# Cosine attention and a GELU layer on one core: a new split of one batch's fill, and two row reductions one step sooner

## The chip, the cores and the metric

The kernel runs on one core of a Trainium2 chip. The core has a matrix engine (TensorE, PE in the profile), a vector engine (VectorE, DVE), an engine for tabulated functions (ScalarE, ACT), a general engine (GpSimd, POOL) and a queue engine (SyncE, SP) that here issues transfers. Each engine takes its own list of instructions in order, and waits on semaphores where an instruction needs another engine's result. The metric is the time of one execution on the device in microseconds; of several executions the median counts. Before the change five executions took 416.24 to 417.19 us, median 416.77 us.

## The reference

Eight batches of 12 heads, 448 positions, 64 numbers a head. Queries and keys are divided by their length, the scores by tau (0.1), then softmax and the product with v. The result, 3584 rows of 768, goes through a layer of 2048 with the exact GELU and back to 768.

```python
q_n = q / (np.linalg.norm(q, axis=-1, keepdims=True) + 1e-06)
k_n = k / (np.linalg.norm(k, axis=-1, keepdims=True) + 1e-06)
scores = np.matmul(q_n, k_n.transpose(0, 1, 3, 2)) / tau
attn = np.exp(scores - np.max(scores, axis=-1, keepdims=True))
attn = attn / (np.sum(attn, axis=-1, keepdims=True) + 1e-09)
x = np.matmul(attn, v)          # (8, 12, 448, 64) -> (3584, 768)
h = x @ w_in                    # (3584, 2048)
g = 0.5 * h * (1.0 + erf(h / sqrt(2)))
out = g @ w_out                 # (3584, 768)
```

## The kernel before

**Units of work.** Four heads of one batch are a quad; there are three quads to a batch and 24 in all, numbered through. The first batch (b = 0) has quads 0 to 2, the second (b = 1) 3 to 5, the third 6 to 8. A list of units holds quad 0 in two halves and then each quad whole, so that unit u + 4 with u = 4 in the second batch means "up to and with quad 6", and u + 5 "up to and with quad 7".

**What a quad goes through.** `load_qk` (issued on SP, four buffers) brings q and k in float32. `square` on GpSimd multiplies them with themselves (two buffers `sq`). `reduce` (L165, VectorE) sums the squares of each row into `nq`; quads 6 and 7 share one `nq` tile, and so do the later steps on it. `logs` and `roots` (ScalarE) take the root as exp(0.5 ln), `inverses` (GpSimd, then VectorE, L192) the inverse, `scale` (GpSimd, L208) multiplies it into q and k and makes bfloat16, and `transposes` turns the result: for most quads by a transposing transfer issued on SP (L220). Then come seven passes of `scores` (PE, L246, four matmuls each, into one of three pairs of PSUM banks called st0, st1, st2) and `exps` (ScalarE, L253, one activation each), which also free the pair again. `both` finishes a quad: `sums` (PE, L275, into a single PSUM bank), `turned` (VectorE, L297, tile `tr`), `inverted` and `spread` (VectorE, L309 to L318), `values` (PE, L289), `normalise` (VectorE, L323, tile `x`).

**The layer behind it.** `first(b)` multiplies the batch's 448 rows with w_in (PE, L649, tiles `hp`) and takes the GELU (ScalarE, L685). The product with w_out is cut into pieces: a piece is one matmul of 384 columns (L352, tile `op`), 16 pieces make one half of an output tile, and the sixteenth also issues its copy out of PSUM on VectorE (L356, tile `ot`), after the second half the store on SP too. These pieces are a `fill`: they are kept and put between the passes of the next batch's attention, to give PE work while ScalarE takes exponentials. The second batch's attention has 96 pieces, of three output tiles: first halves of tiles 0, 1, 2, then second halves of 0, 1, 2. Below they are ot0, ot1, ot2, in that order twice.

**Banks.** Two single PSUM banks, `mm0` and `mm1`, are taken in turn by each new `op` tile and by the first `hp` tiles of `first`. From the second batch on `sums` takes the bank whose turn is next, without passing the turn on; so the tile that comes after takes the same bank, and must wait until `turned` has read the sums.

**The order around the change.** It is written out by hand in `attention(b, fill)`: `run()` issues the next part of the fill by the numbers of `plan`, `visit(b, pairs)` issues passes of scores and exponentials into the named pairs, and `upto(f, n)` issues step f for all units below n that have not had it yet. In the second batch the order is:

- (at the end of `first(0)`: three passes), run 1, scale and transposes of quad 5, loads, square of quad 6, three passes
- run 2, three passes
- run 3, a load, two passes, square of quad 7
- run 4, three passes, `both` of quad 3, loads, two passes, reduce of quad 6
- run 5, three passes, `both` of quad 4, two passes, reduce of quad 7, logs and roots of quads 6 and 7
- run 6, `both` of quad 5, inverses, and then `first(1)`

In the later batches the same code runs, but `first(b - 1)` has already reduced up to and with unit u + 3, so that only one reduction is left for attention, where the first of its two `upto(reduce, ...)` calls issues it.

Of the kernel before, what the change touches and what calls it, by code (L numbers as in the profile page):

```python
# [16 lines left out]
def kernel(  # L17
# [151 lines left out]
    def logs(n):  # L169
        nq = nq_t.pop(n)  # L170
        ln_t[n] = nrm.tile(list(nq.shape), F32, tag="lq", name=f"lq{n}")
        nc.scalar.activation(ln_t[n], nq, AF.Ln, bias=tiny)

    def roots(n):
        ln = ln_t.pop(n)
        if n <= NQ:
            sr_t[n] = root2[n % len(root2)][:, :math.prod(shapes[n])]
            nc.scalar.activation(sr_t[n][:, :, 0], ln.rearrange("p j i s c -> p (j i s c)"), AF.Exp, scale=0.5)
        else:
            sr_t[n] = nrm.tile(list(ln.shape), F32, tag="sr", name=f"sr{n}")  # L180
            nc.scalar.activation(sr_t[n], ln, AF.Exp, scale=0.5)  # L181

    def inverses(n):
        sr = sr_t.pop(n)
        shape = [128] + shapes[n]
        se = nrm.tile(shape, F32, tag="se", name=f"se{n}")
        if n <= NQ:
            nc.vector.tensor_reduce(se.rearrange("p j i s c -> p (j i s c)"), sr, mybir.AxisListType.X, ALU.add)
        else:
            nc.gpsimd.tensor_scalar(se, sr, 1e-6, None, ALU.add)  # L190
        rn = nrm.tile(shape, F32, tag="rn", name=f"rn{n}")
        nc.vector.reciprocal(rn, se)  # L192
        rn_t[n] = rn
# [42 lines left out]
    def scores(g, banks, p=None):  # L236
        qkT = qkT_t[g]
        if p is None:
            p = st_turn[0]
            st_turn[0] ^= 1  # L240
        st = pair(p, f"st{g}_{banks[0][1]}")
        for n, (s, c) in enumerate(banks):
            rows = slice(64 * s, 64 * (s + 1))
            for h in range(2):
                cols = slice(64 * h, 64 * (h + 1))
                nc.tensor.matmul(st[cols, n, :S], lhsT=qkT[rows, 1, c, cols], rhs=qkT[rows, 0, :, cols],  # L246
                                 start=True, stop=True, tile_position=(64 * s, 64 * h))
        st_t[g, banks[0]] = st

    def exps(g, banks):  # L250
        st, m = st_t.pop((g, banks[0])), len(banks)
        pt = ptp.tile([128, 2, S], BF16, tag="pt", name=f"pt{g}_{banks[0][1]}")
        nc.scalar.activation(pt[:, :m], st[:, :m, :S], AF.Exp, scale=inv_tau)  # L253
        for n, (s, c) in enumerate(banks):
            pt_t[g, s, c] = pt[:, n]
# [69 lines left out]
    def both(g, p):  # L325
        sums(g)
        turned(g)
        inverted(g)
        spread(g, 0)
        spread(g, 1)  # L330
        values(g, p=p)
        normalise(g, 0)
        normalise(g, 1)
# [9 lines left out]
    def second_pieces(sb, t, ni):  # L343
        state = {}

        def mm(kf):
            if kf == 0:
                state["ps"] = mm_tile(f"op{sb}_{t}_{ni}")
                if ni == 0:
                    ot_t[sb, t] = op_.tile([128, d_model], F32, tag="ot", name=f"ot{sb}_{t}")  # L350
            ps, ot = state["ps"], ot_t[sb, t]
            nc.tensor.matmul(ps[:, :NH], lhsT=g_t[sb][:, kf, t * 128:(t + 1) * 128],  # L352
                             rhs=wo[:, kf, ni * NH:(ni + 1) * NH],
                             start=(kf == 0), stop=(kf == KF - 1))
            if kf == KF - 1:
                nc.vector.tensor_copy(ot[:, ni * NH:(ni + 1) * NH], ps[:, :NH])  # L356
                if ni == 1:
                    store(sb, t, ot, 0, d_model, (nc.sync, nc.sync))

        return [lambda kf=kf: mm(kf) for kf in range(KF)]  # L360
# [33 lines left out]
    def upto(f, n, last=None):  # L394
        last = {load_qk: NG, load_v: NV, root: len(groups), load_wi: 4, load_wo: 4}.get(f, NU)
        while done.get(f, 0) < min(n, last):
            done[f] = done.get(f, 0) + 1
            f(done[f] - 1)
# [180 lines left out]
    def visit(b, pairs):  # L579
        for p in pairs:  # L580
            n, c = passes[at.get(b, 0)]
            at[b] = at.get(b, 0) + 1
            scores(b * NQ + n, ((0, c), (1, c)), p)
            exps(b * NQ + n, ((0, c), (1, c)))

    def attention(b, fill):
        fill = list(fill)
        plan = {96: (16, 14, 16, 18, 16, 16), 128: (20, 18, 20, 22, 32, 16)}[len(fill)]
        parts = iter(plan)

        def run():
            for _ in range(next(parts)):
                fill.pop(0)()

        x_t[b] = xp.tile([128, KD, S], BF16, tag="x", name=f"x{b}")
        g0, u = b * NQ, b * NQ + 1
        run()
        upto(scale, u + 3)
        upto(transposes, u + 3)
        if b == 1:  # L600
            upto(load_qk, g0 + NQ + 2)
            upto(square, u + 4)
        visit(b, (0, 1, 2))
        if b > 1:
            upto(scale, u + 4)
            upto(transposes, u + 4)
        run()
        visit(b, (0, 1, 2))
        run()
        upto(load_qk, g0 + NQ + 3)  # L610
        visit(b, (0, 1) if b <= 2 else (0, 1, 2))
        upto(square, u + 5)
        run()
        visit(b, (0, 1, 2))
        both(g0, 0)
        upto(load_v, b + 3)
        upto(load_qk, g0 + NQ + 4)
        visit(b, (1, 2))
        upto(reduce, u + 4 + (b > 1))
        run()  # L620
        visit(b, (1, 2, 0))
        both(g0 + 1, 1)
        visit(b, (2, 0))
        upto(reduce, u + 5)
        n = 2 * b + 4
        if n < len(groups):
            logs(n)
            roots(n)
        run()
        both(g0 + 2, 2)  # L630
        if n < len(groups):
            inverses(n)
            done[root] = n + 1
            if b > 1:
                visit(b + 1, (0, 1))
# [72 lines left out]
    fill = []  # L708
    for b in range(B):
        if b == 0:  # L710
            attention_first()
            acc.close()
            third.append(ctx.enter_context(tc.tile_pool(name="ps_third", bufs=1, space=bass.MemoryType.PSUM)))
        else:
            attention(b, fill)
        first(b)
        sb, hf = divmod(b, 2)
        todo = [(t, ni) for t in (range(3) if hf == 0 else range(3, 7)) for ni in range(2)]
        if b == 0:
            todo.sort(key=lambda x: x[1])  # L720
        tail = [2 * S // 128 - 1] if b == B - 1 else []
        fill = [f for t, ni in todo if t not in tail for f in second_pieces(sb, t, ni)]
        fill += [f for t in tail for f in last_pieces(sb, t)]
# [37 lines left out]
```

## Time and profile before

The profiled execution took 416.24 us; the span on the page, from the first to the last instruction, is 414.4 us. The granted clock of PE was 1.000 over the span.

| | us |
|---|---|
| median of five executions | 416.77 |
| the profiled execution | 416.24 |
| its span | 414.4 |
| PE busy | 406.3 |
| ACT busy | 246.2 |
| DVE busy | 188.6 |
| POOL busy | 166.9 |
| one reduce of a whole quad (L165), in the chain | 1.92 |
| one square of a whole quad (L156) | 3.17 |
| one exponential pass (L253), mean | 0.917 |
| 96 pieces (L352) in the chain | 15.60 |
| q and k loads on SP, issue to landing, median | 6.9 and 8.8 |

How to read the lines: in an order of time a line gives the start and the length in us, the engine, the source line and operation, the tile written, an arrow, the tiles read, the shapes, and how many instructions of the kind stand together; in square brackets is the idle time of the engine before them and what ended it. In a list of waits a line gives who waited for whom: us in total, times, the longest. A busy PE is not a PE at its peak; its idle time is what a better order can take away.

### The profile page before, as it was taken

What the parts mean: (1) busy time and instruction counts of PE and PEld (TensorE: products, weight loads), DVE (VectorE), ACT (ScalarE), POOL (GpSimd) and SP (SyncE); (2) the same over time, 40 slices, a digit from 0 to 9 for tenths busy, and PEclk for the clock granted to TensorE, in tenths of its full rate; (3) what the DMA queues carried; (4) which work ended last, traced back from release to release, by engine and by line L of the source; (5) the groups of instructions that cost most, each with busy time, mean ns of one, the idle gap of its engine ahead of it and who ended that gap; (6) DMA issues with size and microseconds to landing.
All of it is one profiled execution on the core that took longest, in us unless ns stands there. A gap on an engine that the chain in (4) does not pass through costs nothing.

```text
span 414.4 us, 8256 instructions
## 1 busy us (share of the span) xinstructions
PE 406.3 (98%) x3506; PEld 212.3 (51%) x3506; DVE 188.6 (45%) x379; ACT 246.2 (59%) x358; POOL 166.9 (40%) x113
## 2 busy tenths in 40 slices
PE   7999999899999999999999999999999999999996
PEld 3445545455555555555555555555555555545564
DVE  5687116923268221943148431783118611481021
ACT  6995686546746567754764648755665467754300
POOL 4998605074820919044630537217370233000000
PEclk9999999999999999999999999999999999999999
DMA  8999999625396405935296232965078120510033
GB/s 289 262 260 206 203 241 300 136 57 133 57 225 205 115 19 92 278 91 125 30 201 217 65 107 46 210 195 133 2 144 217 40 44 2 120 40 2 0 78 77
DMA packets 66516, 54.53 MB, mean 132 GB/s; under 512 B 38576, under 2 KB 61488, under 8 KB 66480
## 3 DMA queue, kind: packets, MB, share of 16 engines
q1 hardware_dynamic: 53984, 41.79, 38.3%
q0 software_dynamic: 12112, 11.80, 17.9%
q8 instruction: 27, 0.44, 0.4%
q10 hardware_dynamic: 384, 0.43, 0.4%
q14 instruction: 9, 0.07, 0.1%
HBM read 45.61 MB, written 11.01 MB: 137 GB/s over the span
## 4 chain that ended last, share of the span: by engine, by line
PE 92%; DVE 4%; ACT 2%; DMA 1%; issue 0%; POOL 0%; DVEq 0%
PE hp L649 35%; PE op L352 33%; PE st L246 9%; PE o L289 7%; PE sm L275 4%; PE op L367 1%; DVE nq L165 1%; PE sm L266 1%; ACT pt L253 1%; PE tp L225 1%; DMA qk<-in_q_dram 1%; DVE x L323 1%; PE spin L403 0%; DVE tr L297 0%; DVE tr L309 0%
## 5 line engine op out<-in xcount | busy, mean ns | idle before, releaser
L253 ACT ACTIVATE pt<-st 128x896 bf16<-128x896 f32 x168 | 142.8, 917 | 66.5 <-PE st L246 66.2
L649 PE MATMUL hp<-x,wi 128*128 128x448 bf16 x768 | 146.8, 353 | 1.2 <-DVE tr L297 1.2
L352 PE MATMUL op<-wo,g 128*128 128x384 bf16 x864 | 147.8, 326 | 0.0
L352 PEld LDWEIGHTS <-g 128*128 128x128 bf16 x864 | 81.5, 98 | 62.1 <-issue 10.7
L649 PEld LDWEIGHTS <-wi 128*128 128x128 bf16 x768 | 74.5, 98 | 72.5 <-issue 4.0
L685 ACT ACTIVATE g<-hp 128x448 bf16<-128x448 f32 x128 | 65.9, 545 | 68.3 <-PE hp L649 68.0
L208 POOL TENSOR_TENSOR qkb<-qk,rn 128x896 bf16<-128x896 f32 (+1 forms) x49 | 79.7, 1652 | 38.0 <-DVE rn L192 37.9
L356 DVE COPY ot<-op 128x384 f32<-128x384 f32 x54 | 29.6, 548 | 101.6 <-PE op L352 101.6
L165 DVE TENSOR_REDUCE nq<-sq 128x28 f32<-128x1792 f32 (+2 forms) x30 | 48.8, 1636 | 53.1 <-POOL sq L156 50.4
L156 POOL TENSOR_TENSOR sq<-qk 128x1792 f32<-128x1792 f32 (+1 forms) x22 | 66.5, 3037 | 14.0 <-DMA qk<-in_k_dram 14.0
L190 POOL TENSOR_SCALAR se<-sr 128x28 f32<-128x28 f32 (+1 forms) x14 | 4.3, 310 | 127.6 <-ACT sr L181 127.5
L246 PE MATMUL st<-qkT 64*64 64x448 bf16 x672 | 48.0, 358 | 0.8 <-ACT pt L253 0.4
L289 PE MATMUL o<-pt,v 64*64 64x448 bf16 x672 | 36.9, 352 | 0.0
L246 PEld LDWEIGHTS <-qkT 64*64 64x64 bf16 x672 | 18.5, 105 | 24.7 <-issue 16.3
L318 DVE STREAM_TRANSPOSE rs<-rc 128x448 f32<-128x448 f32 x48 | 28.1, 623 | 0.8
L323 DVE TENSOR_TENSOR x<-o,rs 128x448 bf16<-128x448 f32 x48 | 27.0, 599 | 1.0 <-DVE rs L318 0.5
L289 PEld LDWEIGHTS <-v 64*64 64x64 bf16 x672 | 17.7, 106 | 17.0 <-issue 8.4
L192 DVE RECIPROCAL rn<-se 128x28 f32<-128x28 f32 (+2 forms) x18 | 6.8, 376 | 42.8 <-POOL se L190 42.6
L297 DVE STREAM_TRANSPOSE tr<-sm 128x448 f32<-128x448 f32 x24 | 15.5, 646 | 14.2 <-PE sm L275 11.1
L275 PE MATMUL sm<-pt,ones 128*32 128x448 bf16 (+1 forms) x336 | 17.8, 332 | 0.0
L309 DVE TENSOR_REDUCE tr<-tr 32x28 f32<-32x28 f32 x84 | 16.4, 196 | 1.6
L275 PEld LDWEIGHTS <-ones 128*32 128x32 bf16 x336 | 6.8, 95 | 9.0 <-issue 7.2
(43 smaller groups left out, 118.1 us busy)
## 6 DMA issues: line engine op xcount, KB each, us to landing
out_dram<-ot SPq DMA_DIRECT2D x54, 192.0 KB, 3.3
qk<-in_q_dram SPq DMA_DIRECT2D x23, 448.0 KB, 6.9
qk<-in_k_dram SPq DMA_DIRECT2D x23, 448.0 KB, 8.8
v<-in_v_dram POOLq DMA_DIRECT2D x7, 672.0 KB, 12.2
wi<-in_moe_w_in_dram POOLq DMA_DIRECT2D x8, 384.0 KB, 13.9
wo<-in_moe_w_out_dram POOLq DMA_DIRECT2D x4, 768.0 KB, 14.1
qk<-in_q_dram SPq DMA_DIRECT2D x2, 224.0 KB, 3.4
v<-in_v_dram POOLq DMA_DIRECT2D x1, 448.0 KB, 8.2
```

The source lines that it names most:

```text
L156: eng.tensor_tensor(sq[:, part], t[:, part], t[:, part], ALU.mult)
L165: nc.vector.tensor_reduce(nq[:, part], sq[:, part], mybir.AxisListType.X, ALU.add)
L208: eng.tensor_tensor(qkb[:, i, :, s0:s1].rearrange("p c s d -> p s c d"), t[:, i, s0:s1], rn[:, i].to_broadcast([128, s1 - s0, C, D]), ALU. ...
L246: nc.tensor.matmul(st[cols, n, :S], lhsT=qkT[rows, 1, c, cols], rhs=qkT[rows, 0, :, cols], start=True, stop=True, tile_position=(64 * s, 6 ...
L253: nc.scalar.activation(pt[:, :m], st[:, :m, :S], AF.Exp, scale=inv_tau)
L275: nc.tensor.matmul(bank_t[g, "sm"][r:r + 32, cols], lhsT=ones, rhs=pt_t[g, s, c][:, cols], start=(c < 2), stop=(c >= C - 2), tile_position ...
L289: nc.tensor.matmul(bank_t[g, h][cols, :S], lhsT=v_t[g][rows, s, c, :], rhs=pt_t[g, s, c][rows], start=(c == 0), stop=(c == C - 1), tile_po ...
L323: nc.vector.tensor_tensor(x_t[b][:, 2 * n + h, :], bank_t.pop((g, h))[:, :S], rs_t.pop((g, h)), ALU.mult)
L352: nc.tensor.matmul(ps[:, :NH], lhsT=g_t[sb][:, kf, t * 128:(t + 1) * 128], rhs=wo[:, kf, ni * NH:(ni + 1) * NH], start=(kf == 0), stop=(kf ...
L356: nc.vector.tensor_copy(ot[:, ni * NH:(ni + 1) * NH], ps[:, :NH])
L649: nc.tensor.matmul(hps[m], lhsT=wi[:, kd, m * 128:(m + 1) * 128], rhs=x_t[b][:, kd, :], start=(kd == 0), stop=(kd == KD - 1))
L685: nc.scalar.activation(g_t[sb][:, m, hf * S:(hf + 1) * S], hps.pop(m), AF.Gelu)
```

## The change

Two edits in `attention`. The fill of the second batch is split 20, 13, 14, 17, 16, 16 instead of 16, 14, 16, 18, 16, 16; batches with 128 pieces, and the other batches with 96, keep their numbers. And the row sums of squares: `upto(reduce, u + 4)` is called ahead of `upto(square, u + 5)`, before the fourth run, and `upto(reduce, u + 5)` where the first of the two calls stood; the last call falls away. In the second batch quad 6 is so reduced between the copies of ot1 and ot2 (first halves), and quad 7 where quad 6 was, between quad 3's `normalise` and the second copy of ot1. In the later batches the new call has nothing left to issue, and the other issues the same as before at the same place.

```diff
     def attention(b, fill):
         fill = list(fill)
-        plan = {96: (16, 14, 16, 18, 16, 16), 128: (20, 18, 20, 22, 32, 16)}[len(fill)]
-        parts = iter(plan)
+        if len(fill) == 128:
+            parts = iter((20, 18, 20, 22, 32, 16))
+        else:
+            parts = iter((20, 13, 14, 17, 16, 16) if b == 1 else (16, 14, 16, 18, 16, 16))
...
         visit(b, (0, 1) if b <= 2 else (0, 1, 2))
+        upto(reduce, u + 4)
         upto(square, u + 5)
         run()
         visit(b, (0, 1, 2))
...
         visit(b, (1, 2))
-        upto(reduce, u + 4 + (b > 1))
+        upto(reduce, u + 5)
         run()
         visit(b, (1, 2, 0))
         both(g0 + 1, 1)
         visit(b, (2, 0))
-        upto(reduce, u + 5)
```

## The prediction

> **What bounds the kernel now.** I read the page's first two parts, then TensorE's (PE's) waits, then the order of time in the second batch's attention, where every edit acts, engine by engine.
>
> ```profile
> PE 406.3 (98%) x3506; PEld 212.3 (51%) x3506; DVE 188.6 (45%) x379; ACT 246.2 (59%) x358; POOL 166.9 (40%) x113
> ...
> PE 92%; DVE 4%; ACT 2%; DMA 1%; issue 0%; POOL 0%; DVEq 0%
> ```
>
> PE is busy for 406.3 of 414.4 us, and the chain that ended last is 92% PE. A change can only gain what PE waits. TensorE's waits in the whole span:
>
> ```profile
> PE spin L403 <- DVE root L89: 1.9, 1, 1.9
> PE hp L649 <- DVE tr L297: 1.2, 1, 1.2
> PE st L246 <- ACT pt L253: 0.4, 1, 0.4
> ```
>
> The first is the start. The other two both lie in the second batch (46 to 84 us); after 81.09 us PE waits for nothing. In order of time, PE first:
>
> ```profile
> 54.70 0.72 PE L246 MATMUL st<-qkT 64*64 64x448 bf16 x8
> 55.85 0.38 PE L246 MATMUL st<-qkT 64*64 64x448 bf16 x4 [0.43 <-ACT pt L253]
> 56.17 2.45 PE L352 MATMUL op<-wo,g 128*128 128x384 bf16 x14
> ...
> 65.48 0.76 PE L246 MATMUL st<-qkT 64*64 64x448 bf16 x12
> ```
>
> and from the third quad's sums on:
>
> ```profile
> 78.40 1.52 PE L289 MATMUL o<-pt,v 64*64 64x448 bf16 x28
> 81.09 3.19 PE L649 MATMUL hp<-x,wi 128*128 128x448 bf16 x16 [1.17 <-DVE tr L297]
> ```
>
> So after its first fill PE waits for the third exponential, and at the end of the attention for VectorE's transpose of the last sums (tr5; quads are numbered through, so the second batch has 3, 4, 5 and the third batch begins with 6, 7). VectorE (DVE):
>
> ```profile
> 62.99 0.56 DVE L356 COPY ot<-op 128x384 f32<-128x384 f32 x1 [2.65 <-PE op L352]
> 65.59 0.56 DVE L356 COPY ot<-op 128x384 f32<-128x384 f32 x1 [2.04 <-PE op L352]
> 67.07 0.65 DVE L297 STREAM_TRANSPOSE tr<-sm 128x448 f32<-128x448 f32 x1 [0.93 <-PE sm L275]
> ...
> 78.02 2.00 DVE L165 TENSOR_REDUCE nq<-sq 128x28 f32<-128x1792 f32 x1
> 79.94 0.54 DVE L356 COPY ot<-op 128x384 f32<-128x384 f32 x1
> 80.40 0.63 DVE L297 STREAM_TRANSPOSE tr<-sm 128x448 f32<-128x448 f32 x1
> ```
>
> VectorE has slack up to 67 us and then runs without a pause to tr5; the reductions of quads 6 and 7 (71.37 and 78.02 us) stand in that stretch. GpSimd (POOL), which makes what they reduce:
>
> ```profile
> 61.18 3.17 POOL L156 TENSOR_TENSOR sq<-qk 128x1792 f32<-128x1792 f32 x1 [11.56 <-DMA qk<-in_k_dram]
> 66.81 3.17 POOL L156 TENSOR_TENSOR sq<-qk 128x1792 f32<-128x1792 f32 x1 [2.45 <-DMA qk<-in_k_dram]
> ```
>
> The squares of quad 6 end at 64.35 us (61.18 + 3.17): their k arrives late. This line decides the forecast.
>
> **Part one, the fills.** The first run goes from 16 to 20 pieces; the sums after each run go from 16, 30, 46, 64 to 20, 33, 47, 64. A piece is one matmul with 384 columns, 0.1625 us (96 take 15.60 us in the chain). PE would come to the scores at 54.70 + 4 × 0.1625 = 55.35 us. The third pair of scores needs the third exponential, which ends at 55.81 us whatever PE does (53.27 + 2.54, after a table load that nothing here moves), so it starts at 55.85 as before, and the second run at about 56.2 as before, with four pieces more behind it: 0.65 us gained. One small price: quad 4's transposed tile lands at 46.36 + 12.3 = 58.66 us, its first scores would move from 58.85 to 58.68, and may lose up to 0.1 us, before a point that will turn out to have slack. With 64 pieces done after four runs either way, PE would come to the sums of quad 3 (sm3) at 66.24 - 0.65 = 65.59 us. Nothing else is moved past a queue by the fills; the eviction of the second piece group (ot1) falls into run two, at some 58.3 us instead of 59.78.
>
> **Part two, the reductions.** On VectorE the built order becomes: copy ot1, reduce 6, copy ot2, copy ot0 (second half), tr3 to x3, reduce 7, copy ot1, tr4 to x4, copy ot2, tr5. Quad 7's reduction takes the old place of quad 6's, and the place at 78 us falls empty: VectorE's unbroken stretch loses 1.92 us (the chain's figure for one). Quad 6's goes behind the ot1 copy, where VectorE arrives at 58.9 us and finds the squares missing until 64.35.
>
> Queued behind it is the ot2 copy (ready at some 62.1 us now, when piece 48 ends), then ot0's. Does a ready copy pass a reduction that waits? In the third batch a reciprocal waited 4.64 us for POOL; the piece group copied next ended on PE at about 102.7 (100.03 + 16 × 0.1625 + pipeline), and its copy ran right behind the reciprocal:
>
> ```profile
> 104.87 0.50 DVE L192 RECIPROCAL rn<-se 128x56 f32<-128x56 f32 x1 [4.64 <-POOL se L190]
> 105.29 0.49 DVE L356 COPY ot<-op 128x384 f32<-128x384 f32 x1
> ```
>
> So a ready copy stands behind a waiting one. Who waits for the ot2 copy: sm3. The two single PSUM banks alternate, sm3 takes the bank that ot2's pieces filled, and in the built program its first matmul waits for exactly that copy. The sum: 64.35 + 0.03 (handing over, as at 39.23 to 39.26) + 1.92 (reduce) + 0.56 (copy) + 0.06 (release, as from tr5's end at 81.03 to 81.09) = 66.92 us. sm3 started at 66.24 before; it starts 0.68 later, and waits 66.92 - 65.59 = 1.33 us. The first wait is not removed, it has moved here, and all that the fills gained is gone.
>
> From there PE, VectorE and ScalarE run in lockstep as before, 0.68 later. PE ends the values of quad 5 at 78.40 + 1.52 + 0.68 = 80.60. VectorE: tr3 67.75, x3 ends 72.12, reduce 7 to 74.04 (its squares end at 69.98: ready), copy 0.47, tr4 to x4 4.26 (73.83 to 78.09 before), copy 0.47, tr5 0.63: 79.87 us. That is 0.73 before PE comes, so hp starts at 80.60 instead of 81.09. **Net: -0.49 us.** Check by waits: before, 0.85 lost round 55 us (54.70 to 56.24 for 0.69 us of scores) and 1.17 at 81; afterwards 0.20 and 1.33; 2.02 - 1.53 = 0.49.
>
> On the other queues: the store of ot0 on SP waits for its copy, 66.15 to some 67.35, and with it the load of quad 9 behind it, from 67.40 to 68.6; it lands 6.3 us after its issue, by 76, and POOL squares that quad after 95 us (second of the two squares from 91.88): 19 us of cover. The logarithms of quads 6 and 7 and the table load, which waited 3.51 us for reduce 7, come some 3 us sooner, and the scaling on POOL (85.29) and the transposes (88.65) about a microsecond sooner; nothing waited for them. From hp on PE is unbroken to the end, so 0.49 us stays.
>
> The unknown is when k of quad 6 lands in other executions. Its issue at 51.58 took 9.5 us to land, the next quad's k 5.7, the transposes before and after it 12.3 and 11.9. With 5.7 the squares would be there before VectorE: full gain, 2.02 - 0.20 = 1.82 us. With 12.3 all would be 2.8 later: 2.3 us slower than before. I take 9.5, since what stands in the queue ahead of it is untouched by the change.
>
> A stall of 1.33 us is longer than any after the start here; the 1.17 us wait left the granted clock at 1.00 in its stretch (81.00 to 99.40 us). The Trainium skill (TensorE: Matmul & The Clock Gate, Part 1: The HAM clock gate) halves the clock after an idle window of some 3.4 us, so it gives no loss here either; were one window at half speed caught, an estimate from that page is 1.7 us, and the sum would turn to 1.2 slower. No run here shows it.
>
> **Rivals.** (1) The squares of quad 6 are ready sooner than in this execution, and much of both waits is really gone. Each tenth sooner is a tenth gained, to 1.82 us at most (414.95 us); from 0.34 us sooner on it counts as faster. For it: the following load landed in 5.7 us, and DMA times scatter. Against: the transposes ahead of it. A typical case, 0.6 us sooner, gives 415.7. (2) The ending on the other side: k of quad 6 lands later, behind the transposes, and sm3 is held for longer than both old waits. Place: sm3; price: one for one; it decides from 0.49 us later (no gain), and from 1.32 later it is slower by 0.2%. At 2.0 us later: 418.3. Against: of SP's transfers in this stretch only the transposes took that long. (3) The gain is given back: something in the next stage holds PE at its old time, 416.77. Against: the trace has no wait of PE there at all, and everything that feeds it comes sooner.
>
> **How the numbers follow.** The profiled execution took 416.24 us for a span of 414.4; the median is 416.77, 0.53 above. The sum of -0.49 is made on the span (413.9) and carried to the median: 416.28, say 416.3. 0.2% is 0.83 us, about what a measurement of this kernel can tell from no change. Chances: forecast 0.52, its own range 415.95 to 416.8 (the landing within 0.35 or so); rival 1 0.36; rival 2 0.07; rival 3 0.05. So faster 0.36, same 0.57, slower 0.07. The range takes in most of rival 1, up to 1.5 us of gain, and rival 2 to 0.3 us slower: 415.25 to 417.1.
>
> **What would show it.** In the changed kernel: no wait of hp for tr at 81 us; a new wait of sm at L275 for the copy at L356, 1.3 us, about 65.6; on VectorE a reduction that ends at 66.3 with 5.5 us of idle time before it, released by POOL; the wait for the exponential near 55.8 shrunk under 0.1. If that new wait is much smaller, rival 1 holds; if it passes 1.8, rival 2; if sm shows no wait and hp still does, my reading of the VectorE order is wrong.

## The result, and the profile after

The changed kernel took 415.95 us in the median (43 executions, 415.46 to 418.62), the kernel before 416.94 (80 executions, 416.24 to 421.02). The ratio is 0.9972, with a 95% interval of 0.9963 to 0.9980: faster by 0.28%, 1.0 us by the medians and 1.2 by the ratio, where 0.49 us was forecast. The profiled execution of the changed kernel took 415.60 us with a span of 413.8. The profiled execution of the kernel before, 416.24 us, on which the prediction was made, is the fastest of all 80, 0.70 us under their median.

TensorE's waits in the second batch (46 to 84 us), changed kernel; a line is who waited for whom, us in total, times, the longest:

```profile
PE sm L275 <- DVE ot L356: 0.4, 1, 0.4
```

Both old waits are gone, and the one named in the prediction has come in their place: the sums of quad 3 for the copy at L356. Only it is 0.4 us long and not 1.33. TensorE in order of time:

```profile
52.78 3.42 PE L352 MATMUL op<-wo,g 128*128 128x384 bf16 x20
56.13 0.88 PE L246 MATMUL st<-qkT 64*64 64x448 bf16 x12
56.95 2.29 PE L352 MATMUL op<-wo,g 128*128 128x384 bf16 x13
...
65.61 0.76 PE L246 MATMUL st<-qkT 64*64 64x448 bf16 x12
66.80 0.85 PE L275 MATMUL sm<-pt,ones 128*32 128x448 bf16 x16 [0.43 <-DVE ot L356]
...
80.44 3.77 PE L651 MATMUL hp<-x,wi 128*128 128x448 bf16 x19
```

The first fill starts at 52.78 and not at 52.00. Over the fourteen profiles of this document it starts at 52.0 to 53.7 us, with either order in the second batch, and from hp (the first matmul of `first(1)`) to the end of the span every one of them takes 333.3 to 333.4 us. So what differs between them is the start and the stretch from the first fill to hp, and stretches are compared from here on. The second run starts 4.17 us after the first, as before (56.17 - 52.00), with 20 pieces done instead of 16. The twelve scores behind run 4 start 12.83 us after the first fill (before 13.48): 0.65 sooner, as worked out. From the first fill to hp it is 27.66 us; before it was 29.09: 1.43 less, of which the later start of this execution takes 0.78 back in its time. VectorE in order of time:

```profile
59.11 0.56 DVE L356 COPY ot<-op 128x384 f32<-128x384 f32 x1 [2.96 <-PE op L352]
64.26 2.02 DVE L165 TENSOR_REDUCE nq<-sq 128x28 f32<-128x1792 f32 x1 [4.60 <-POOL sq L156]
66.20 1.01 DVE L356 COPY ot<-op 128x384 f32<-128x384 f32 x2
67.70 0.65 DVE L297 STREAM_TRANSPOSE tr<-sm 128x448 f32<-128x448 f32 x1 [0.48 <-PE sm L275]
...
79.11 0.65 DVE L297 STREAM_TRANSPOSE tr<-sm 128x448 f32<-128x448 f32 x1
```

The reduction of quad 6 waits 4.60 us for the squares, the copies of ot2 and ot0 stand behind it as a pair, and tr5 ends at 79.76, 0.68 us before PE gets to hp. The chain that ended last, from the load on, tells it in one piece (start, us, what):

```profile
52.75 8.19 DMA qk<-in_k_dram
...
61.06 3.18 POOL sq L156
64.24 0.02 issue
64.26 2.02 DVE nq L165
66.28 0.48 DVE ot L356
66.76 0.04 issue
66.80 0.85 PE sm L275 x16
```

So what bounds this stage in this execution is the load of quad 6's k, through square, reduction and copy. It landed 8.2 us after its issue; in the execution that the prediction was made on it was 9.5.

### The profile page after: what moved, and what is told of

Its sections match the earlier page's. It is cut to its first block, busy times and chain, and to the rows that moved or that the text cites. A ratio compares the mean times of both kernels' runs of the same rounds, so it can differ in the third digit from the quotient of the medians.

```text
span 413.8 us, 8256 instructions
## 1 busy us (share of the span) xinstructions
PE 406.9 (98%) x3506; PEld 212.4 (51%) x3506; DVE 188.4 (46%) x379; ACT 246.3 (60%) x358; POOL 166.9 (40%) x113
## 4 chain that ended last, share of the span: by engine, by line
PE 89%; POOL 4%; DMA 2%; DVE 2%; ACT 1%; issue 1%; SPq 1%; POOLq 0%
PE op L352 32%; PE hp L651 31%; PE st L246 9%; PE o L289 8%; PE sm L275 4%; POOL qkb L208 2%; PE spin L403 2%; DMA qk<-in_k_dram 2%; POOL sq L156 2%; PE op L367 1%; DVE nq L165 1%; PE sm L266 1%; ACT pt L253 1%; PE tp L225 1%; SPq L220 0%
## 5 line engine op out<-in xcount | busy, mean ns | idle before, releaser
L165 DVE TENSOR_REDUCE nq<-sq 128x28 f32<-128x1792 f32 (+2 forms) x30 | 48.8, 1637 | 57.7 <-POOL sq L156 55.0
L356 DVE COPY ot<-op 128x384 f32<-128x384 f32 x54 | 29.5, 548 | 95.5 <-PE op L352 95.5
L403 PE MATMUL spin<-blank,ident 128*128 128x448 bf16 x34 | 10.3, 449 | 2.2 <-DVE root L89 1.9
## 6 DMA issues: line engine op xcount, KB each, us to landing
v<-in_v_dram POOLq DMA_DIRECT2D x7, 672.0 KB, 12.1
```

Of the source, the lines that this page charges most:

```text
L165: nc.vector.tensor_reduce(nq[:, part], sq[:, part], mybir.AxisListType.X, ALU.add)
```

## The experiments

Each is an edit of the kernel before or of the changed kernel. "Stretch" is from the first fill to hp in the profiled execution; the kernel before beside each median ran on the same chip. Rows one to four, five to eight and nine to twelve were each on one chip. The waits: "ACT" is for the third exponential, "qkT" that of the scores for quad 4's transposed tile, "sm" that of quad 3's sums for the copy of ot2, "hp" that for tr5. The ratios below are to the kernel before, with a 95% interval.

| run | median us | before us | stretch us | PE waits in it |
|---|---|---|---|---|
| changed kernel again | 416.00 | 416.86 | 28.36 | sm 1.14 |
| fill alone | 416.23 | 416.86 | 28.95 | hp 1.17, qkT 0.32 |
| reductions alone | 416.68 | 416.86 | 28.98 | ACT 0.43, sm 0.77 |
| squares ready | 415.42 | 416.86 | 28.98 | qkT 1.59 |
| square twice | 421.07 | 416.99 | 35.05 | qkT 0.69, sm 4.52 |
| reduction past the copy | 415.27 | 416.99 | 27.83 | qkT 0.44 |
| the same, first run 21 | 414.70 | 416.99 | 27.17 | none |
| w_out later | 420.24 | 416.99 | 31.15 | qkT 1.10, sm 2.62 |
| kernel before again | 417.08 | 416.85 | 29.67 | ACT 0.43, qkT 0.38, hp 1.18 |
| before, second run 18 | 416.83 | 416.85 | 29.09 | ACT 0.43, hp 1.17 |
| first run 21 again | 415.12 | 416.85 | 27.08 | none |
| first run 21, second 15 | 414.68 | 416.85 | 27.08 | none |

**The changed kernel again**, without an edit.

> The changed kernel once more, on the chip of the next three. Theory: the sums of quad 3 wait for the copy of ot2 behind the reduction of quad 6, and the load that its squares need lands at about 61 us whatever the start does, so an execution whose PE begins later gains more: 0.5 us under the kernel before in the earliest start, 1.0 to 1.3 in the usual one; median 1.0 under. Rival: the load lands a fixed 9.5 us after its issue, every execution gains 0.5, and the rest of the median is scatter: 0.5 under.

0.86 us under the kernel before by the medians (ratio 0.9988, 0.9974 to 1.0001). Its profile has the same wait with another size: the squares start at 61.59, the first fill at 52.61, and

```profile
67.33 0.85 PE L275 MATMUL sm<-pt,ones 128*32 128x448 bf16 x16 [1.14 <-DVE ot L356]
```

The prediction's sum fits both executions to the hundredth: sm can start 5.74 us after the squares do (3.17 + 0.03 + 1.92 + 0.56 + 0.06), and PE gets there 13.59 us after the first fill. 61.06 + 5.74 = 66.80 and 61.59 + 5.74 = 67.33, both as recorded; the waits 0.43 and 1.13. In two runs below that also have this wait, the reductions alone and w_out later, the squares start at 62.99 and 64.78, and sm at 68.74 and 70.52: the same 5.75 and 5.74.

**The fill alone**, on the kernel before:

```diff
-        plan = {96: (16, 14, 16, 18, 16, 16), 128: ...
+        plan = {96: (20, 13, 14, 17, 16, 16) if b == 1 else (16, 14, 16, 18, 16, 16), 128: ...
```

> The new split of the fill alone, the reductions where they were. Theory: nothing stands ahead of the sums of quad 3, so the 0.65 us of the four earlier pieces stay, the whole stretch down to tr5 comes 0.65 sooner, and the 1.17 us wait of hp for tr5 stays as it is: 0.65 us under the kernel before. Rival, that only the wait for tr5 is worth anything: no change.

0.63 us under the kernel before (ratio 0.9981, 0.9971 to 0.9991): the theory holds, the rival that only the wait for tr5 is worth something falls. The profile shows a price that I had put at 0.1 us at most; two of TensorE's waits:

```profile
PE hp L649 <- DVE tr L297: 1.2, 1, 1.2
PE st L246 <- DMA qkT<-qkb: 0.3, 1, 0.3
```

Quad 4's transposed tile landed 12.7 us after its issue, and its first scores waited for it. With the pipeline behind that wait PE lost 0.52 us, so that in this execution only 0.14 of the 0.65 were left (29.09 to 28.95).

**The reductions alone**, on the changed kernel:

```diff
-            parts = iter((20, 13, 14, 17, 16, 16) if b == 1 else (16, 14, 16, 18, 16, 16))
+            parts = iter((16, 14, 16, 18, 16, 16) if b == 1 else (16, 14, 16, 18, 16, 16))
```

> The moved reductions alone, the fill split as before (16, 14, 16, 18, 16, 16). Theory: the wait for tr5 (1.17 us) goes, and PE comes to the sums of quad 3 0.65 later than in the changed kernel, so the copy of ot2 is late by 0.7 in the earliest start and by nothing in a start 0.8 later: 0.5 to 1.17 us under the kernel before, median 1.0 or so under, that is, about the same as both edits together. Rival, landing a fixed time after issue: 0.5 under, with a 0.68 us wait of sm for the copy in the profile.

0.18 us under the kernel before by the medians (ratio 0.9997, 0.9982 to 1.0013): no difference that can be told. My theory of the late start falls here. The first fill began at 53.39, 1.4 us later than in the first profile of before, and the squares of quad 6 at 62.99, 1.8 later: the load does not land at a fixed time, it moved with the start and more. Over the profiles with the transfers unmoved the squares started 8.3 to 10.2 us after k's issue, with neither a fixed time nor a fixed delay. So the rival's fixed landing falls too, and that the 0.77 us wait of sm is near its 0.68 is chance. TensorE in order of time:

```profile
59.94 1.10 PE L246 MATMUL st<-qkT 64*64 64x448 bf16 x12
...
68.74 0.85 PE L275 MATMUL sm<-pt,ones 128*32 128x448 bf16 x16 [0.77 <-DVE ot L356]
```

The twelve scores behind the second run, quad 4's first among them, took 1.10 us instead of 0.76: the tile landed 12.7 us after its issue, and cost a third of a us that is too short to be listed as a wait. Without it sm would have waited 1.1 us.

**Squares ready**, on the changed kernel: the squares of quad 6 are taken from quad 5's q and k, which are long there. This kernel leaves out quad 6's own lengths and divides by quad 5's; the number of operations is the same.

```diff
-                eng.tensor_tensor(sq[:, part], t[:, part], t[:, part], ALU.mult)
+                src = qk_t[5][:, :, s0:s1] if g == 6 else t
+                eng.tensor_tensor(sq[:, part], src[:, part], src[:, part], ALU.mult)
```

> The changed kernel, but GpSimd squares quad 5's q and k in the place of quad 6's, so that it needs no load that is still on the way; the number of operations is the same, the lengths of quad 6 are those of quad 5. Theory: the squares are done by 54 us, the reduction of quad 6 runs at 59, the copy of ot2 at 62, sm waits for nothing, and both old waits are gone: 1.8 us under the kernel before, 0.5 to 0.9 under the changed one. Rival, that the wait of sm is not what limits the gain: the same time as the changed kernel.

1.44 us under the kernel before, 0.58 under the changed one on the same chip (ratio to before 0.9970, 0.9954 to 0.9986). The interval overlaps that of the changed kernel beside it, so by time alone the two are not told apart; the profile is what shows that the wait of sm is gone, as expected. In the profiled execution, which took 417.42 us and is one of the slowest of its twelve, another took its place: quad 4's tile landed 14.0 us after issue.

```profile
PE st L247 <- DMA qkT<-qkb: 1.6, 1, 1.6
```

**Square twice**, on the changed kernel: GpSimd squares quad 6 two times into the same tile.

```diff
-        for eng, part in parts or ((nc.gpsimd, slice(0, 2)),):
+        for eng, part in parts or ((nc.gpsimd, slice(0, 2)),) * (2 if g == 6 else 1):
```

> The changed kernel, but GpSimd squares quad 6 twice into the same tile, so the squares are ready 3.17 us later. Theory: the wait of sm for the copy of ot2 (0.4 to 1.1 us in the two profiles of the changed kernel) grows by 3.17 to 3.6 to 4.3, and nothing later takes it up: 3.1 us over the changed kernel, about 2.2 over the kernel before. Rival, that the squares are hidden and the wait has another cause: the time of the changed kernel.

4.1 us over the kernel before (ratio 1.0100, 1.0066 to 1.0134), where 2.2 were expected. The wait is as long as expected, 4.52 us, but what follows it is slow; TensorE in order of time:

```profile
71.25 1.50 PE L275 MATMUL sm<-pt,ones 128*32 128x448 bf16 x16 [4.52 <-DVE ot L356]
72.68 2.83 PE L289 MATMUL o<-pt,v 64*64 64x448 bf16 x28
```

16 sums take 1.50 us instead of 0.85 and 28 values 2.83 instead of 1.52. The busy time by stretches says why; behind the five engines stand the granted clock, the transfer engines' share and GB/s:

```profile
65.00:71.20 6.20, 1.74 (x19) 0.75 (x18) 2.48 (x3) 2.54 (x3) 6.12 (x3) 0.87 0.72 259
71.20:73.00 1.80, 1.75 (x20) 0.69 (x23) 0.67 (x3) 0.00 (x0) 1.45 (x2) 0.50 0.08 19
73.00:76.00 3.00, 3.00 (x36) 1.27 (x28) 2.82 (x9) 0.06 (x1) 0.00 (x0) 0.50 0.90 113
76.00:79.00 3.00, 3.00 (x22) 1.51 (x18) 3.00 (x4) 1.67 (x2) 0.00 (x0) 0.93 1.15 280
```

The clock went to 0.50 during the wait and stayed there to 76 us. From sm to hp it took 16.07 us instead of 13.64: 2.43 us for the clock. The first square starts at 62.26; with a second one of 3.17 the sum gives 62.26 + 3.17 + 5.74 = 71.17 for sm, and it started at 71.25. So the squares are on the path, one for one, and the rival that they are hidden falls.

**The reduction past the copy**, on the changed kernel: one piece moves from the fourth run to the third, so that ot2's copy is issued ahead of the reduction.

```diff
-            parts = iter((20, 13, 14, 17, 16, 16) if b == 1 else ...
+            parts = iter((20, 13, 15, 16, 16, 16) if b == 1 else ...
```

> The changed kernel with the fill 20, 13, 15, 16, 16, 16: piece 48 falls into the third run, so the copy of ot2 stands ahead of the reduction of quad 6 on VectorE, and nothing that sm needs waits for the squares. The reduction then ends at about 66.3 and holds up only ot0's copy and tr3, by some 0.3 us, which the slack of VectorE behind it takes up. Theory: no wait of sm, no wait of hp, as with the squares made ready: 1.4 to 1.8 us under the kernel before, 0.6 under the changed one. Rival, that the reduction only hands its delay to tr3 and from there to PE: the time of the changed kernel.

1.72 us under the kernel before (ratio 0.9962, 0.9941 to 0.9984). VectorE in order of time:

```profile
62.77 0.56 DVE L356 COPY ot<-op 128x384 f32<-128x384 f32 x1 [3.47 <-PE op L352]
65.35 2.02 DVE L165 TENSOR_REDUCE nq<-sq 128x28 f32<-128x1792 f32 x1 [2.02 <-POOL sq L156]
67.28 0.55 DVE L356 COPY ot<-op 128x384 f32<-128x384 f32 x1
67.75 0.64 DVE L297 STREAM_TRANSPOSE tr<-sm 128x448 f32<-128x448 f32 x1
```

The copy of ot2 is out 2 us before the squares come, sm starts without a wait at 66.57, and the reduction holds up only ot0's copy and tr3. The reduction waits for its squares as in the changed kernel; only what stands behind it differs. The stretch, 27.83 us, lies between the changed kernel's two, since this execution waits 0.44 us for quad 4's tile, and the interval overlaps the changed kernel's. So the edit is shown to take the wait of sm away; that it alone beats the changed kernel is likely by the medians and not settled.

**The same with a first run of 21** (21, 13, 14, 16, 16, 16), twice.

> As the run before, with the fill 21, 13, 14, 16, 16, 16: piece 48 is again in the third run, and the first run is a piece longer, which covers the 0.15 to 0.2 us that PE still waits for the third exponential. Theory: 0.1 us under the run before, hardly to be told from it by time; in the profile the twelve scores behind the first run take 0.76 us and not 0.88. Rival: the scalar engine is now the later one and nothing is gained.

> The fill 21, 13, 14, 16, 16, 16 of the second call once more, beside the next: 2.0 to 2.3 us under the kernel before if both old waits and the new one are gone (2.02 by the waits of the profile, and what PE waited for quad 4's tile is not mended).

2.29 and 1.73 us under the kernel before (ratios 0.9937, 0.9914 to 0.9960, and 0.9952, 0.9930 to 0.9975). The stretch is 27.17 and 27.08 us, 1.9 to 2.0 under the kernel before's 29.09: the two old waits, 2.02 by the prediction's count, are gone whole. The twelve scores behind the first run take 0.76 us and not 0.88, as expected:

```profile
55.74 0.76 PE L246 MATMUL st<-qkT 64*64 64x448 bf16 x12
```

This version beats both kernels: 19 of its 20 executions took 415.52 us or less, and 2 of the changed kernel's 54.

**W_out later**, on the changed kernel: its last quarter is issued at 47.28 us instead of about 41.

```diff
-            upto(load_wo, 4)
+            upto(load_wo, 3)
...
                 upto(load_qk, 2 * NQ + 1)
+                upto(load_wo, 4)
```

> The changed kernel, but the last quarter of w_out (768 KB, issued at about 40 us) is issued between the scalings of quads 4 and 5, at about 47 us. Theory: the transposed tile of quad 4 and the load of quad 6 share the transfer engines with it, and their landing (12 and 8 to 9 us after issue) comes 1 us or more sooner, so the wait of sm shrinks: 0.3 to 0.8 us under the changed kernel, unless the late quarter itself is awaited at its first use near 63 us. Rival, that the transposes set the pace by themselves: landings as before, the time of the changed kernel.

3.25 us over the kernel before (ratio 1.0066, 1.0036 to 1.0095). My theory was wrong in its sign: k of quad 6 landed 12.2 us after its issue and quad 4's tile 13.5, where the two profiles of the changed kernel have 8.2 and 8.9, and 11.3 and 12.1; sm waited 2.62 us. That the transfers hold each other up is shown by it, and the rival that the transposes set the pace alone falls. The transfer of the quarter itself in the changed kernel (tile and source, times, size, us from issue to landing):

```profile
wo<-in_moe_w_out_dram POOLq DMA_DIRECT2D x1, 768.0 KB, 16.8
```

and here:

```profile
wo<-in_moe_w_out_dram POOLq DMA_DIRECT2D x1, 768.0 KB, 16.6
```

Issued at 40.9 and landed 16.8 us later, at 57.7, the quarter lies beside the transpose of quad 4 (47.14 to 58.4) in the changed kernel already; issued at 47.28 it landed at 63.9, and so lay beside k's transfer (52.44 to 64.6) nearly to its end. In all thirteen other profiles k lands 2.6 to 3.3 us and quad 4's tile 0.2 to 0.8 us after this quarter, while the quarter itself lands anywhere from 4.9 to 8.0 us after k's issue. So the landings of k and of the tile scatter with that of w_out's last quarter. That the quarter can hold them up is what this run shows; whether it makes their scatter in the other runs, or something else delays all three, is open. A run with the quarter issued earlier would tell, and there is none.

**The kernel before again**, without an edit, and **with a second run of 18**:

```diff
-        plan = {96: (16, 14, 16, 18, 16, 16), 128: ...
+        plan = {96: (16, 18, 12, 18, 16, 16) if b == 1 else (16, 14, 16, 18, 16, 16), 128: ...
```

> The kernel before, profiled once more. New theory, after the first runs: the transposed tile of quad 4 lands 12.1 to 14.0 us after its issue and mostly later than in the profiled execution of before, so its first scores wait for it, in the kernel before at full price, in the changed one inside a wait of sm that is there anyway; that is why the median gain is larger than the 0.5 us worked out from the one execution. Expected: PE waits for the transfer of qkT by 0.2 to 0.6 us, beside the 0.43 and the 1.17. Rival, that executions differ by their start alone: no such wait, and the first fill begins 0.5 us or more later than at 52.0.

> The kernel before with the fill 16, 18, 12, 18, 16, 16: the second run four pieces longer, the third four shorter, so quad 4's first scores are asked for 0.65 us later and everything behind the third run at the same place as before. New theory: the wait for quad 4's tile goes, 0.2 to 0.5 us under the kernel before in the median. Rival: the time of the kernel before.

The second profile of the kernel before, an execution of 418.56 us and the slowest of its eleven, has what the theory and its rival both name, the wait for quad 4's tile and a late start (first fill at 53.74); TensorE's waits in the second batch:

```profile
PE hp L649 <- DVE tr L297: 1.2, 1, 1.2
PE st L246 <- ACT pt L253: 0.4, 1, 0.4
PE st L246 <- DMA qkT<-qkb: 0.4, 1, 0.4
```

Its stretch is 29.67, 0.58 longer than in the first profile. Yet asking for the tile 0.65 us later brought nothing in the median, 416.83 beside 416.85 (ratio 0.9996, 0.9982 to 1.0010). So that wait exists, but that it makes the median of the kernel before is not shown.

**First run 21, second run 15** (21, 15, 12, 16, 16, 16):

> The same with 21, 15, 12, 16, 16, 16: the second run two pieces (0.33 us) longer, so quad 4's tile is asked for 0.33 us later, with piece 48 still in the third run. New theory: up to 0.3 us under the run before. Rival: the same.

414.68 beside 415.12 and 416.85 (ratio to before 0.9940, 0.9913 to 0.9967). The stretch is the same 27.08 and neither profile has a wait in it; the difference to the run beside it is not settled. Both are the fastest versions here, 0.5 to 0.6% under the kernel before.

## Why the prediction was right, and where it was not

*What bounds the kernel* held: two waits of PE in the second batch, and nothing after 81 us takes a gain back: every profile takes the same 333.3 to 333.4 us from hp on.

*The fills* held: 0.65 us sooner in front of the sums, and 0.63 by themselves in time. The price that I put on quad 4's tile, at most 0.1 us, was too small: 0.32 to 1.59 us of waiting in six of the twelve profiles of the table, and a third of a us in a seventh. Where sm waits anyway it costs nothing more: with the squares taken twice and with w_out later PE waited 0.69 and 1.10 us for the tile, and sm still started where the squares alone put it.

*The new wait* is there, at the place, on the engine and for the cause that were given; squares made ready take it away, squares made later lengthen it, and the sum from the squares to sm holds to 0.1 us in all five profiles that have the wait. The term that was off is "I take 9.5", the landing of quad 6's k: it took 8.2 and 8.9 us in the two profiles of the changed kernel, so the wait was 0.43 and 1.14 us where 1.33 was worked out, and the stretch shrank by 1.43 and 0.73 us instead of 0.49. As a typical value 9.5 was not bad: over the thirteen profiles with the transfers unmoved k took 8.2 to 10.6 us, 9.4 in the middle. But it was a single draw out of a scatter of more than 2 us, and the reason given for it, that what stands ahead in the queue is untouched, does not keep it at 9.5. The prediction's rival 1 named this case, squares ready sooner and a smaller wait, and its range took it in; its likeliest outcome was a change under 0.2% (0.57, against 0.36 for faster), and the kernel came out 0.28% faster.

*The rest of the median's gain*, some 0.9 to 1.2 us beside 0.49, is not wholly settled. By the prediction's count, 1.82 us less the wait, it asks for a typical wait of 0.6 to 1.0 us, between the 0.43 and 1.14 of the two profiles. By the sum the wait is the time from the first fill to the squares less 7.85 us; that time is 8.3 to 10.0 us over the profiles with the transfers unmoved and 9.2 in the middle, which would give 1.4. Whether k lands sooner in the changed kernel as a rule is not shown by two profiles. Two other explanations were tried: that late starts gain more (fell with the reductions alone) and that the kernel before also pays for quad 4's tile (seen in its second profile, not in the median of the run that took it away).

*Two readings* in the prediction are off without harm. With a landing after 5.7 us the squares would end at about 60.6 us, not before VectorE, which comes at 58.9; the gain would be full even so, since the reduction would end near 62.5, well before sm. And sm started at 66.17 in the line, not at 66.24, where the scores ahead of it end.

*VectorE's slack behind it* held: tr5 was 0.68 us ahead of PE, 0.73 worked out. *The stores* held: the first one 14.46 us after the first fill instead of 14.17, with no wait of PE behind it.

*The clock* held: 1.00 after the waits of 0.43 and 1.14. With the squares taken twice, in a wait of 4.52 us, it fell to 0.50 some 2.9 us after the last matmul's end (66.74 to 69.6, an estimate from the mean of 0.87 over 65.00 to 71.20), and 2.43 us were lost. The Trainium skill (TensorE: Matmul & The Clock Gate, Part 1: The HAM clock gate) gives half speed after an idle window of about 3.4 us; here it came about half a us sooner than that, and the loss was above the 1.7 us that I estimated from the page for one window.

## What to carry to other kernels

Moving a step to where its engine is idle is free only if the step can start there: ask when its input lands, and what is queued behind it meanwhile. Here one piece of fill, moved so that a copy stands in front of a reduction that waits, took the wait behind it away, and with one piece more in the first run the gain was 1.7 to 2.3 us instead of 1.0. And a term that rests on the landing of one transfer needs more than one execution: its scatter of 2.4 us was five times the forecast gain.

## What had not been expected of the hardware

A transfer issued 6 us later (768 KB of w_out) made others beside it land later: k of quad 6 took 12.2 us from its issue, where the other profiles have 8.2 to 10.6. In those others it landed 2.6 to 3.3 us after that transfer did, and that transfer 4.9 to 8.0 us after k's issue. And a wait of 4.5 us cost TensorE another 2.4 us, since the granted clock stood at 0.50 until about 5 us after the wait's end; 2.62 us of waiting (w_out later) left it at full speed, 28 values taking 1.52 us as ever.
